# A chunked recurrence with routing beside it: update and bonus ahead of the state's product, logits a step later, the zero fill in four parts

## The chip, the cores and the metric

The kernel runs on 1 core of one Trainium2 chip. The metric is the device time of one execution in microseconds; the time before is the median of three runs. One execution was also profiled, and its trace is what is read below.

## The reference

Three layers follow each other, all in fp32. The first is a linear recurrence over 768 time steps for 4 batches and 8 heads of 48 dimensions:

```python
for t in range(S):
    cur = np.einsum('bhd,bhe->bhde', u[None] * kt, vt)
    y[:, :, t] = np.einsum('bhd,bhde->bhe', rt, state + cur)
    state = w[None, :, :, None] * state + np.einsum('bhd,bhe->bhde', kt, vt)
```

Its output, as 3072 tokens of 384 values, goes through a routed mixture of 8 experts (a token is computed if its product with w_skip is positive, by the expert with the largest logit, weighted by the softmax's value), and then through a soft mixture: logits x @ phi to 32 slots, a softmax over the tokens to gather slot inputs, 8 experts of 4 slots each, and a softmax over the slots to give the result back to the tokens.

## The kernel before, in words

**Steps of the recurrence.** The loop over i from 0 to 23 (L973 to L1047) takes one chunk of 128 tokens of one batch at a time: 6 chunks of time by 4 batches, the batch running faster. All 8 heads are in one step, as 4 pairs, a pair's heads at partitions 0 and 64. The functions below are called with the step whose data they take, j:

- load(j), called three steps ahead: SyncE issues two loads of r and k (rkb, 192 KB each) and one of k and v (kvt, 384 KB), into five buffers each.
- prep(j) and prepk(j), one step ahead: VectorE scales r and k (rks, L616), GpSimd makes their product pd (L618) and the decayed keys kt (L624).
- scores(j): TensorE multiplies keys and queries into sc (L633), a PSUM tile with one buffer, and sums pd over the head into dt (L636); ScalarE copies dt to dts (L638). These are the bonus rows, the term with u.
- inter(j), a step late: TensorE multiplies the queries with the state, which ScalarE has laid out as sbd (stateb, L676), into yp (L702).
- trx(j), two steps late: TensorE transposes the finished y (yt) through the same PSUM tag "t" that dt uses (L721); ScalarE copies it to x (L722), the token-major table.
- bonus(j): TensorE transposes dts (L656) into the PSUM tile ud, one buffer, which also holds the update and the routing's sums.
- upd(j): TensorE forms keys times values, the chunk's addition to the state (L649), into ud. There is none for the last time chunk, steps 20 to 23.
- amask(j): VectorE masks sc into at (L681) and copies the bonus rows onto its diagonal (copy_predicated, L688).
- state(j): VectorE adds the update to the decayed state (L668; GpSimd has made the decayed state, L667).
- av(j), a step late: TensorE multiplies at with the values into yp (L712); ScalarE copies it to yt (L715).

**Routing.** Every four steps a group of four tiles (all batches of a time chunk) is finished and is routed during the following steps, with rc, rb = divmod(i - 5, 4). At rb 0 route1 multiplies yt with the gate, skip and phi weights (lgt, L744) and ScalarE copies the logits; at rb 1 route2 transposes them (lgp, L804) and route2b finds the chosen expert with eight small VectorE operations (L820 to L837) and ScalarE's exponential (L831); at rb 3 route3 counts tokens with six small matmuls into ud, weave and count compute gate weights and places (VectorE, L861 to L888), and route4 stores the logits of the soft mixture: lt on GpSimd, and ltm with the maximum's negative as bias on ScalarE (mn, L905, and four activations, L907). scat(j) is GpSimd's indirect DMA of x rows to the experts' buffer xs_d. At steps 21 to 23 the maximum of ltm over the tokens is taken (cmax, colmax, the matmul of rows), subtracted (lx, L1007, L1029) and exponentiated (L1030). Groups of the last steps follow behind the loop.

**Order.** The schedule is manual: every engine executes its instructions in the order in which the code issues them. SyncE's queue also issues the zero fill of xs_d (L1034, one DMA of 3096 KB at step 2) and the experts' weights (wload at steps 8, 11 and 14, two of 768 KB each).

**Behind the recurrence.** The experts (L1119 on) load rows of xs_d, transpose them and run in fp32 parts on TensorE (L1140 to L1167) until some 350 us; the soft mixture follows.

Of the kernel before, what the change touches and what calls it, by code (L numbers as in the profile page):

```python
# [19 lines left out]
P = 128  # L20
NC_ = S // P
NT = B * NC_
DM = H * D
# [438 lines left out]
def tile_main(ctx, tc, rk, kv, wu, wcat, phi, w1, w2, v1, v2, r_in, k_in, v_in, w_in, u_in, wcn, out, dbg=None, force=False):  # L462
# [92 lines left out]
    def constants(i):  # L555
        if i == 3:
            nc.vector.tensor_scalar(tri, mask, float(E), None, op0=ALU.mult)
        if i == 4:
            nc.vector.tensor_scalar(eb2[0:1], eb_i[0:1], 1.0 / E, None, op0=ALU.mult)
            nc.vector.memset(eb2[32:33], -float(NOROW // E))  # L560
            nc.vector.tensor_scalar(w8, eb_i, -1.0, float(E), op0=ALU.mult, op1=ALU.add)
        if i == 5:
            nc.vector.memset(x[:, :, DM : DM + 1], 1.0)
            nc.vector.memset(ohacc, 0.0)
        if i == 6:
            nc.vector.tensor_reduce(sel4, ident.rearrange("p (q s) -> p s q", q=4), axis=AX.X, op=ALU.add)
            nc.vector.tensor_scalar(pio, pi_i, float(E), None, op0=ALU.mult)

# [57 lines left out]
    def scores(j):  # L626
# [11 lines left out]
        nc.scalar.copy(t["dts"], dt_)  # L638

    def upd(j):  # L640
        t = T[j]
# [9 lines left out]
    def bonus(j):  # L651
        t = T[j]
        t["ud"] = ps.tile([P, 352], F32, tag="ud", name=f"ud{j}")
        t["dk"] = t["ud"][:, 0 : P + 4 * E]
        t["dtk"] = t["ud"][:, 0:P]
        nc.tensor.transpose(t["dtk"], t["dts"], ident)  # L656

# [240 lines left out]
    def route4(g):  # L898
        c, (j0, nb) = g, GR[g]
        sh = [P, nb, E]  # L900
        r = RT.pop(c)
        lg, m = r["lg"], r["m"]
        nc.gpsimd.tensor_copy(lt[:, j0 : j0 + nb, :], lg[:, :, 9:41])
        mn = rt.tile([P, nb, 1], F32, tag="mn", name=f"mn{c}")
        nc.scalar.mul(mn, m, NEG)  # L905
        for b in range(nb):
            nc.scalar.activation(ltm[:, j0 + b, :], lg[:, b, 9:41], AF.Identity, bias=mn[:, b, :])  # L907

# [63 lines left out]
    if True:  # L972
        for i in range(NT):  # L973
# [4 lines left out]
            if i == 0:  # L978
                prep(0)
                for hf in range(2):  # L980
                    r0 = 64 * hf
                    nc.vector.tensor_copy(usel[r0 : r0 + D, :, hf : hf + 1], wt[r0 : r0 + D, 1, :].rearrange("p (a o) -> p a o", o=1))
            scores(i)
            if i > 0:
                inter(i - 1)
                stateb(i - 1)
            if i > 1:
                trx(i - 2)
            bonus(i)
            if i == 0:  # L990
# [5 lines left out]
                for b in range(B):  # L996
                    nc.gpsimd.memset(sbd[b], 0.0)
            elif i + 1 < NT:
                prep(i + 1)
                prepk(i + 1)  # L1000
            if rok and rb == 1:
                route2(rc)
            if rok and (rb == 3 or i == 23):
                route3(rc, place=T[i]["dk"][:, P:])
            if i == 22:
                mrt = rows(nc, cn, "t", rt, pa, "u", mcs[:, 0:1])
                nc.vector.tensor_copy(lx[:, 0:1, :], mrt)  # L1007
            upd(i)
            amask(i)
            state(i)  # L1010
            if i > 0:
                av(i - 1)
            if rok and rb == 0:
                route1(rc)
            if i == 23:
                route1(5)
            if rok and rb == 1:
                route2b(rc)
            if i == 23:
                weave("gpgpgp", g=gates(4), p=places(4))  # L1020
            if rok and rb == 3:
                weave("gpgpgp", g=gates(rc), p=places(rc))
                count(rc)
                route4(rc)
            if i == 21:
                nc.vector.tensor_reduce(cmax, ltm[:, 0:16, :].rearrange("t b s -> t s b"), axis=AX.X, op=ALU.max)
                colmax(nc, cn, "t", pa, "u", mcs[:, 0:1], fourfold(nc, "t", rt, cmax))
            if i == 22:
                nc.vector.tensor_sub(ltm[:, 0:16, :], ltm[:, 0:16, :], lx[:, 0:1, :].to_broadcast([P, 16, 32]))  # L1029
                nc.scalar.activation(ltm[:, 0:16, :], ltm[:, 0:16, :], AF.Exp)  # L1030
            if i in (8, 11, 14):
                wload((i - 8) // 3)
            if i == 2:
                nc.sync.dma_start(out=xs_d.rearrange("(a p) n -> p a n", p=P), in_=zt.rearrange("p (o n) -> p o n", o=1).to_broadcast([P, NSLOT // P, XW]))  # L1034
            if 3 <= i < 7:
                constants(i)
            if i == 4:
                nc.gpsimd.tensor_copy(x[:, :, DM + 2 : DM + 3].bitcast(I32), row_i.rearrange("p (j o) -> p j o", o=1))
            if i == 6:
                wok = rt.tile([PR, 4], F32, tag="wok", name="wok")  # L1040
# [3 lines left out]
                wmn = mk.tile([PR, 1], BF16, name="wmn")  # L1044
                nc.vector.tensor_reduce(wmn, wok2, axis=AX.X, op=ALU.min)
            if i > 8:
                scat(i - 9)  # L1047
# [54 lines left out]
        cnt = mk.tile([P, E + 1, 1], F32, name="cnt")  # L1102
        nc.vector.tensor_copy(cnt.rearrange("p e o -> p (e o)"), cntp)
        rst.close()
        pst.close()
# [428 lines left out]
```

## Time and profile before

| what | value |
|---|---|
| median of three runs | 379.0 us (377.95 to 379.61) |
| profiled execution, its own time | 377.18 us |
| its span | 375.4 us |
| mean granted clock of TensorE | 0.958 |
| busy: TensorE, VectorE, ScalarE, GpSimd | 344.7, 250.4, 160.6, 118.8 us |
| moved by DMA | 84.36 MB, 225 GB/s |
| zero fill of xs_d | 1 DMA of 3096 KB |
| first expert matmul (L1140) | 164.51 us |

The profile's page gives sums over the span; a stage is read with the stage table (busy time of each engine in a stretch), the table of waits (an engine's idle time in front of an instruction, put down to what released it) and the timeline (instructions in order of their start, with the idle time before them in brackets). Starts are in us from the beginning of the span.

### The profile page before, as it was taken

What the parts mean: (1) busy time and instruction counts of PE and PEld (TensorE: products, weight loads), DVE (VectorE), ACT (ScalarE), POOL (GpSimd) and SP (SyncE); (2) the same over time, 40 slices, a digit from 0 to 9 for tenths busy, and PEclk for the clock granted to TensorE, in tenths of its full rate; (3) what the DMA queues carried; (4) which work ended last, traced back from release to release, by engine and by line L of the source; (5) the groups of instructions that cost most, each with busy time, mean ns of one, the idle gap of its engine ahead of it and who ended that gap; (6) DMA issues with size and microseconds to landing.
All of it is one profiled execution on the core that took longest, in us unless ns stands there. A gap on an engine that the chain in (4) does not pass through costs nothing. (4 is left out here: it accounts for less than half of the span.)

```text
span 375.4 us, 8403 instructions
## 1 busy us (share of the span) xinstructions
PE 344.7 (92%) x3313; PEld 280.3 (75%) x3313; DVE 250.4 (67%) x496; ACT 160.6 (43%) x357; POOL 118.8 (32%) x149
## 2 busy tenths in 40 slices
PE   8998979999899878899999999999999999999860
PEld 3676866868777566369999999999899999734350
DVE  7895987896969874646748484748565865426660
ACT  1253424444534332425555564645555543311270
POOL 7962846776754505420012020202020202020000
PEclk9999989999999998589999999999999999999995
DMA  7999998699943101296977887777867466849485
GB/s 181 278 329 245 240 296 202 226 223 318 230 125 124 41 2 44 67 320 222 326 269 245 275 272 245 259 262 266 294 239 241 110 233 199 308 148 399 173 315 196
DMA packets 45696, 84.36 MB, mean 225 GB/s; under 512 B 3961, under 2 KB 26831, under 8 KB 45648
## 3 DMA queue, kind: packets, MB, share of 16 engines
q1 hardware_dynamic: 42320, 78.29, 66.6%
q0 software_dynamic: 2800, 5.28, 4.8%
q8 instruction: 28, 0.46, 0.5%
q10 hardware_dynamic: 528, 0.16, 0.2%
q14 instruction: 20, 0.16, 0.1%
HBM read 72.94 MB, written 13.30 MB: 230 GB/s over the span
## 5 line engine op out<-in xcount | busy, mean ns | idle before, releaser
L1140 PE MATMUL hp<-xhl,wa 128*128 128x256 f32 x192 | 48.6, 290 | 0.2 <-ACT xhl L1130 0.2
L1141 PE MATMUL hp<-xhl,wa 128*128 128x256 f32 x192 | 47.2, 282 | 0.0
L1165 PE MATMUL yp<-wb,hh 128*128 128x384 f32 x128 | 45.3, 354 | 0.0
L953 DVE TENSOR_TENSOR wa<-w,wa 128x768 fp32r<-128x768 f32 x32 | 30.5, 954 | 22.1 <-ACT wa L965 20.9
L1166 PE MATMUL yp<-wb,hh 128*128 128x384 f32 x128 | 43.1, 337 | 0.0
L1167 PE MATMUL yp<-wb,hlo 128*128 128x384 f32 x128 | 43.1, 337 | 0.0
L1198 POOL DMA_INDIRECT lt_d<-lsr,id x16 | 17.5, 1095 | 80.2 <-ACT xhl L1130 56.7
L688 DVE COPY_PREDICATED at<-ident,ud 128x1024 f32<-128x1024 int32 x24 | 31.6, 1315 | 12.1 <-PE ud L649 6.9
L618 POOL TENSOR_TENSOR pd<-rkb 112x512 f32<-112x512 f32 x24 | 30.6, 1277 | 24.8 <-DMA rkb<-in_rk_dram 10.1
L1140 PEld LDWEIGHTS hp<-xhl,wa 128*128 128x128 f32 x192 | 36.4, 189 | 0.5 <-ACT xhl L1130 0.5
L1141 PEld LDWEIGHTS hp<-xhl,wa 128*128 128x128 f32 x192 | 36.5, 190 | 0.0
L891 POOL DMA_INDIRECT xs_d<-x,idx x24 | 24.1, 1004 | 29.2 <-ACT yt L715 12.6
L633 PEld LDWEIGHTS sc<-rks 48*128 48x128 f32 x384 | 23.3, 187 | 13.0 <-DVE at L681 7.9
L633 PE MATMUL sc<-rks 48*128 48x128 f32 x384 | 27.9, 285 | 5.5 <-DVE at L681 5.4
L953 DVE TENSOR_TENSOR wb<-w,wb 128x768 fp32r<-128x768 f32 x32 | 30.5, 954 | 3.2 <-ACT wb L965 3.2
L616 DVE TENSOR_TENSOR rks<-rkb,prk 112x1024 f32<-112x1024 f32 x24 | 29.1, 1213 | 5.2 <-DMA rkb<-in_rk_dram 4.9
L681 DVE TENSOR_TENSOR at<-sc,mask 128x1024 f32<-128x1024 f32 x24 | 29.2, 1218 | 3.0 <-PE sc L633 3.0
L965 ACT CAST wb<-w 128x768 fp32r<-128x768 f32 x32 | 26.8, 838 | 9.0 <-PE yp L1167 5.1
L1150 ACT ACTIVATE hh<-hp 128x512 fp32r<-128x512 f32 x32 | 19.1, 597 | 26.2 <-PE hp L1143 26.2
L1151 DVE SCALAR_TENSOR_TENSOR hlo<-hp,hh 128x512 fp32r<-128x512 f32 x32 | 22.0, 688 | 12.4 <-ACT hh L1150 12.4
L1143 PE MATMUL hp<-xhl,wa 128*128 128x256 f32 x192 | 28.3, 283 | 0.0
L712 PE MATMUL yp<-at,kvt 128*48 128x128 f32 (+1 forms) x384 | 28.0, 281 | 0.0
(330 smaller groups left out, 697.1 us busy)
## 6 DMA issues: line engine op xcount, KB each, us to landing
w<-in_w_dram SPq DMA_DIRECT2D x32, 768.0 KB
v<-in_v_dram SPq DMA_DIRECT2D x29, 768.0 KB
rkb<-in_rk_dram SPq DMA_DIRECT2D x48, 192.0 KB
kvt<-in_kv_dram SPq DMA_DIRECT2D x24, 384.0 KB
out_dram<-ob SPq DMA_DIRECT2D x5, 768.0 KB
xs_d<-zt SPq DMA_DIRECT2D x1, 3096.0 KB
xg<-xs_d POOLq DMA_DIRECT2D x6, 387.0 KB, 5.2
x<-in_v_dram SPq DMA_DIRECT2D x2, 768.0 KB
```

The source lines that it names most:

```text
L616: nc.vector.tensor_mul(rks, rkt, prk)
L618: nc.gpsimd.tensor_mul(t["pd"], rkt[:, 0], rkt[:, 1])
L633: nc.tensor.matmul(sc[:, hf, p, :], ks[r0 : r0 + D, p, :], rs[r0 : r0 + D, p, :], start=True, stop=True)
L681: nc.vector.tensor_mul(at, t["sc"], mask.rearrange("s (a o t) -> s a o t", a=1, o=1).to_broadcast([P, 2, 4, P]))
L688: nc.vector.copy_predicated(at, ident_i.rearrange("s (a o t) -> s a o t", a=1, o=1).to_broadcast([P, 2, 4, P]), t["dtk"].rearrange("s (p o ...
L953: nc.vector.tensor_sub(lv, sl, hv.bitcast(F32))
L1140: nc.tensor.matmul(hp[:, f, :], hi[:, k, fs], xh[:, k, :], start=(k == 0 and f == 0), stop=False)
L1141: nc.tensor.matmul(hp[:, f, :], lo[:, k, fs], xh[:, k, :], start=False, stop=False)
L1143: nc.tensor.matmul(hp[:, f, :], hi[:, k, fs], xl[:, k, :], start=False, stop=(k == 2 and f == 1))
L1165: nc.tensor.matmul(YP[e][bl], hh[:, f, bs], hi[:, f, :], start=st, stop=False)
L1166: nc.tensor.matmul(YP[e][bl], hh[:, f, bs], lo[:, f, :], start=False, stop=False)
L1167: nc.tensor.matmul(YP[e][bl], hlo[:, f, bs], hi[:, f, :], start=False, stop=en)
```

## The change

1. upd and bonus are called right behind scores, ahead of inter, stateb and trx; newud takes the tile. route3 follows bonus, and so does route1.
2. route1 moves from rb 0 to rb 1 and route2 to the end of that step; route2b moves to rb 2; weave and count stay at rb 3; route4 moves to the next step, rb 0 of the following group. The masked logits become one VectorE operation.
3. The zero fill is issued in four parts, at steps 2 to 5.
4. sel4 and pio (constants) move from step 6 to behind the experts' counts, the weight checks (wok, wmn) from step 6 to step 23.
5. Steps 21 to 23: the maximum is taken behind route4 of group 3 and route1 of group 4; rows stands ahead of the mask, its copy behind it, and the subtraction and exponential move from step 22 to step 23.

```diff
--- before.py
+++ after.py
@@ -562,9 +562,6 @@
         if i == 5:
             nc.vector.memset(x[:, :, DM : DM + 1], 1.0)
             nc.vector.memset(ohacc, 0.0)
-        if i == 6:
-            nc.vector.tensor_reduce(sel4, ident.rearrange("p (q s) -> p s q", q=4), axis=AX.X, op=ALU.add)
-            nc.vector.tensor_scalar(pio, pi_i, float(E), None, op0=ALU.mult)
 
     zt = kp.tile([P, XW], F32, name="zt")
     nc.gpsimd.memset(zt, 0.0)
@@ -637,6 +634,12 @@
         t["dts"] = wk.tile([P, P], F32, tag="dts", name=f"dts{j}")
         nc.scalar.copy(t["dts"], dt_)
 
+    def newud(j):
+        t = T[j]
+        t["ud"] = ps.tile([P, 352], F32, tag="ud", name=f"ud{j}")
+        t["dk"] = t["ud"][:, 0 : P + 4 * E]
+        t["dtk"] = t["ud"][:, 0:P]
+
     def upd(j):
         t = T[j]
         if j < NT - B:
@@ -649,11 +652,7 @@
                     nc.tensor.matmul(up[64 * hf : 64 * hf + m, p, :], kt[:, h * D : h * D + m], kvt[:, 1, h * D : h * D + D], start=True, stop=True)
 
     def bonus(j):
-        t = T[j]
-        t["ud"] = ps.tile([P, 352], F32, tag="ud", name=f"ud{j}")
-        t["dk"] = t["ud"][:, 0 : P + 4 * E]
-        t["dtk"] = t["ud"][:, 0:P]
-        nc.tensor.transpose(t["dtk"], t["dts"], ident)
+        nc.tensor.transpose(T[j]["dtk"], T[j]["dts"], ident)
 
     def state(j):
         if j >= NT - B:
@@ -896,15 +895,11 @@
         tc.add_to_no_dep_group("rows", ins.ins)
 
     def route4(g):
-        c, (j0, nb) = g, GR[g]
-        sh = [P, nb, E]
-        r = RT.pop(c)
+        j0, nb = GR[g]
+        r = RT.pop(g)
         lg, m = r["lg"], r["m"]
         nc.gpsimd.tensor_copy(lt[:, j0 : j0 + nb, :], lg[:, :, 9:41])
-        mn = rt.tile([P, nb, 1], F32, tag="mn", name=f"mn{c}")
-        nc.scalar.mul(mn, m, NEG)
-        for b in range(nb):
-            nc.scalar.activation(ltm[:, j0 + b, :], lg[:, b, 9:41], AF.Identity, bias=mn[:, b, :])
+        nc.vector.scalar_tensor_tensor(ltm[:, j0 : j0 + nb, :], m.to_broadcast([P, nb, 32]), NEG, lg[:, :, 9:41], op0=ALU.mult, op1=ALU.add)
 
 
     wraw, WS = {}, {}
@@ -981,12 +976,19 @@
                     r0 = 64 * hf
                     nc.vector.tensor_copy(usel[r0 : r0 + D, :, hf : hf + 1], wt[r0 : r0 + D, 1, :].rearrange("p (a o) -> p a o", o=1))
             scores(i)
+            newud(i)
+            if i > 0:
+                upd(i)
+            bonus(i)
+            if rok and (rb == 3 or i == 23):
+                route3(rc, place=T[i]["dk"][:, P:])
+            if rok and rb == 1 and rc < 4:
+                route1(rc)
             if i > 0:
                 inter(i - 1)
                 stateb(i - 1)
             if i > 1:
                 trx(i - 2)
-            bonus(i)
             if i == 0:
                 decays()
                 warm(ps, "y", 7)
@@ -995,54 +997,55 @@
                 prepk(1)
                 for b in range(B):
                     nc.gpsimd.memset(sbd[b], 0.0)
+                upd(0)
             elif i + 1 < NT:
                 prep(i + 1)
                 prepk(i + 1)
-            if rok and rb == 1:
-                route2(rc)
-            if rok and (rb == 3 or i == 23):
-                route3(rc, place=T[i]["dk"][:, P:])
             if i == 22:
+                route2(4)
                 mrt = rows(nc, cn, "t", rt, pa, "u", mcs[:, 0:1])
+            amask(i)
+            if i == 22:
                 nc.vector.tensor_copy(lx[:, 0:1, :], mrt)
-            upd(i)
-            amask(i)
             state(i)
             if i > 0:
                 av(i - 1)
-            if rok and rb == 0:
-                route1(rc)
+            if i == 21:
+                route4(3)
+                route1(4)
+                nc.vector.tensor_reduce(cmax, ltm[:, 0:16, :].rearrange("t b s -> t s b"), axis=AX.X, op=ALU.max)
+                colmax(nc, cn, "t", pa, "u", mcs[:, 0:1], fourfold(nc, "t", rt, cmax))
+            elif rb == 0 and 1 <= rc < 4:
+                route4(rc - 1)
+            if rok and rb == 1 and rc < 4:
+                route2(rc)
+            if i == 22:
+                route2b(4)
+            if rok and rb == 2 and rc < 4:
+                route2b(rc)
             if i == 23:
                 route1(5)
-            if rok and rb == 1:
-                route2b(rc)
-            if i == 23:
                 weave("gpgpgp", g=gates(4), p=places(4))
-            if rok and rb == 3:
-                weave("gpgpgp", g=gates(rc), p=places(rc))
-                count(rc)
-                route4(rc)
-            if i == 21:
-                nc.vector.tensor_reduce(cmax, ltm[:, 0:16, :].rearrange("t b s -> t s b"), axis=AX.X, op=ALU.max)
-                colmax(nc, cn, "t", pa, "u", mcs[:, 0:1], fourfold(nc, "t", rt, cmax))
-            if i == 22:
                 nc.vector.tensor_sub(ltm[:, 0:16, :], ltm[:, 0:16, :], lx[:, 0:1, :].to_broadcast([P, 16, 32]))
                 nc.scalar.activation(ltm[:, 0:16, :], ltm[:, 0:16, :], AF.Exp)
-            if i in (8, 11, 14):
-                wload((i - 8) // 3)
-            if i == 2:
-                nc.sync.dma_start(out=xs_d.rearrange("(a p) n -> p a n", p=P), in_=zt.rearrange("p (o n) -> p o n", o=1).to_broadcast([P, NSLOT // P, XW]))
-            if 3 <= i < 7:
-                constants(i)
-            if i == 4:
-                nc.gpsimd.tensor_copy(x[:, :, DM + 2 : DM + 3].bitcast(I32), row_i.rearrange("p (j o) -> p j o", o=1))
-            if i == 6:
                 wok = rt.tile([PR, 4], F32, tag="wok", name="wok")
                 nc.vector.tensor_scalar(wok, wt[:, 0, :], WLO, None, op0=ALU.is_ge)
                 wok2 = rt.tile([PR, 4], F32, tag="wok", name="wok2")
                 nc.vector.scalar_tensor_tensor(wok2, wt[:, 0, :], WHI, wok, op0=ALU.is_le, op1=ALU.mult)
                 wmn = mk.tile([PR, 1], BF16, name="wmn")
                 nc.vector.tensor_reduce(wmn, wok2, axis=AX.X, op=ALU.min)
+            if rok and rb == 3:
+                weave("gpgpgp", g=gates(rc), p=places(rc))
+                count(rc)
+            if i in (8, 11, 14):
+                wload((i - 8) // 3)
+            if 2 <= i < 6:
+                q = NSLOT // 4
+                nc.sync.dma_start(out=xs_d[(i - 2) * q : (i - 1) * q].rearrange("(a p) n -> p a n", p=P), in_=zt.rearrange("p (o n) -> p o n", o=1).to_broadcast([P, q // P, XW]))
+            if 3 <= i < 7:
+                constants(i)
+            if i == 4:
+                nc.gpsimd.tensor_copy(x[:, :, DM + 2 : DM + 3].bitcast(I32), row_i.rearrange("p (j o) -> p j o", o=1))
             if i > 8:
                 scat(i - 9)
         for j in range(15, 20):
@@ -1101,6 +1104,8 @@
         nc.tensor.matmul(cntp[:, E : E + 1], ones[:PR, :], wmn, start=True, stop=True)
         cnt = mk.tile([P, E + 1, 1], F32, name="cnt")
         nc.vector.tensor_copy(cnt.rearrange("p e o -> p (e o)"), cntp)
+        nc.vector.tensor_reduce(sel4, ident.rearrange("p (q s) -> p s q", q=4), axis=AX.X, op=ALU.add)
+        nc.vector.tensor_scalar(pio, pi_i, float(E), None, op0=ALU.mult)
         rst.close()
         pst.close()
         pl = qst.enter_context(tc.tile_pool(name="pl", bufs=1, space=PSUM))
```

**Where instructions move.** TensorE in step 14, before, up to the first two of the update's eight matmuls. The number in a name is its step; sc are the scores, dt the bonus sums, yp the state's product, trp the transposes of y, ud the bonus (from dts) and the update (from kt), lgp the transposes of the logits.

```order
L633 MATMUL sc14_1248<-rks14_1204 128x128 x8
L636 MATMUL dt14_1257<-pd14_1206,usel_120 32x128 x4
L702 MATMUL yp13_1264<-rks13_1115,sbd1_193 112x128 x4
L721 MATMUL trp12_1271<-ident_126,yt3_1232 128x112 x4
L656 MATMUL ud14_1277<-ident_126,dts14_1262 128x128
L804 MATMUL lgp2_1285<-ident_126,lgs2_1235 128x128 x4
L649 MATMUL ud14_1277<-kvt14_1011,kt14_1208 64x48
L649 MATMUL ud14_1277<-kvt14_1011,kt14_1208 48x48
```

And TensorE in the same step now, from the last two of the update's eight matmuls on; sc14, dt14 and the other six stand right ahead of them, in this order:

```order
L652 MATMUL ud14_1242<-kvt14_988,kt14_1199 64x48
L652 MATMUL ud14_1242<-kvt14_988,kt14_1199 48x48
L655 MATMUL ud14_1242<-ident_126,dts14_1240 128x128
L743 MATMUL lgt2_1252<-yt2_898,wcs_118 64x512 x4
L701 MATMUL yp13_1259<-rks13_1119,sbd1_193 112x128 x4
L720 MATMUL trp12_1266<-ident_126,yt3_1215 128x112 x4
L711 MATMUL yp13_1259<-at13_1201,kvt13_907 48x128 x8
L803 MATMUL lgp2_1293<-ident_126,lgs2_1253 128x128 x4
```

All eight matmuls of the update and the bonus now stand between dt and the state's product yp13; group 2's logits (lgt2) have come from the end of step 13 into step 14, and their transposes from the middle of the step to its end.

ScalarE around the copy of the bonus rows of step 13 (dts13), before:

```order
L715 COPY yt2_910<-yp11_1100 112x4x128
L905 ACTIVATE mn1_1160<-lgp1_963 128x4
L907 ACTIVATE ltt_162<-lg1_968,mn1_1160 128x32 x4
L638 COPY dts13_1187<-dt13_1182 128x128
L676 COPY sbd0_192<-sp0_188 48x4x48 x2
L722 COPY x_159<-trp11_1196 128x384
```

And now:

```order
L714 COPY yt2_898<-yp11_1106 112x4x128
L635 COPY dts13_1170<-dt13_1165 128x128
L675 COPY sbd0_192<-sp0_188 48x4x48 x2
L721 COPY x_159<-trp11_1189 128x384
L714 COPY yt3_1215<-yp12_1182 112x4x128
```

mn and the four masked logits no longer stand ahead of dts13; they are one VectorE operation at the end of step 13.

SyncE's queue from the loads of step 5 on (rkb and kvt; kvt's number is its step), before:

```order
L503 DMA rkb0_106<-in_rk_dram 48x1024 x2
L505 DMA kvt5_335<-in_kv_dram 128x768
L1034 DMA xs_d_124<-zt_167 128x16x387
L503 DMA rkb1_107<-in_rk_dram 48x1024 x2
L505 DMA kvt6_398<-in_kv_dram 128x768
L503 DMA rkb2_108<-in_rk_dram 48x1024 x2
L505 DMA kvt7_461<-in_kv_dram 128x768
L503 DMA rkb3_109<-in_rk_dram 48x1024 x2
```

And now:

```order
L503 DMA rkb0_106<-in_rk_dram 48x1024 x2
L505 DMA kvt5_335<-in_kv_dram 128x768
L1044 DMA xs_d_124<-zt_167 128x4x387
L503 DMA rkb1_107<-in_rk_dram 48x1024 x2
L505 DMA kvt6_398<-in_kv_dram 128x768
L1044 DMA xs_d_124<-zt_167 128x4x387
L503 DMA rkb2_108<-in_rk_dram 48x1024 x2
L505 DMA kvt7_462<-in_kv_dram 128x768
L1044 DMA xs_d_124<-zt_167 128x4x387
L503 DMA rkb3_109<-in_rk_dram 48x1024 x2
L505 DMA kvt8_531<-in_kv_dram 128x768
L1044 DMA xs_d_124<-zt_167 128x4x387
```

The zero fill xs_d, 16 blocks in one DMA, is four DMAs of 4 blocks, each with one step's loads behind it.

## Rows read from the trace of the kernel before

Columns of a stage table's row: stretch, its us; busy us of PE, PEld, DVE, ACT and POOL, each with the number of its instructions; PEclk, the granted clock; the DMA engines' share; GB/s.

**Rows 1.** Stage table, first scores of steps 5, 9, 17, 19, 22, then experts

```profile
29.48:55.08 25.60, 21.96 (x295) 17.93 (x294) 18.78 (x35) 9.03 (x23) 13.14 (x15) 0.93 1.05 263
55.08:76.92 21.84, 20.59 (x295) 16.61 (x295) 18.04 (x33) 9.94 (x28) 15.45 (x18) 1.00 0.80 214
98.77:110.95 12.18, 11.31 (x151) 8.72 (x150) 8.17 (x16) 5.76 (x17) 8.34 (x10) 1.00 0.60 161
110.95:128.63 17.68, 15.16 (x192) 11.45 (x191) 16.55 (x30) 7.59 (x21) 8.17 (x9) 1.00 0.27 89
128.63:142.49 13.86, 11.76 (x127) 9.30 (x126) 9.11 (x23) 3.71 (x9) 1.58 (x2) 0.88 0.04 14
170.00:350.00 180.00, 180.00 (x1361) 159.33 (x1363) 111.09 (x206) 86.65 (x167) 24.47 (x31) 1.00 0.75 255
```

**Rows 2.** Table of waits, 8 to 165 us: total, times, longest

```profile
PE trp L721 <- ACT dts L638: 5.8, 6, 1.7
PE sc L633 <- DVE at L681: 5.4, 6, 2.1
DVE rks L616 <- DMA rkb<-in_rk_dram: 4.9, 2, 4.2
DVE lx L1007 <- PE mrpt L97: 2.3, 1, 2.3
DVE xhl L1131 <- ACT xhl L1130: 3.6, 1, 3.6
```

**Rows 3.** Timeline, TensorE: start, us, instructions, idle before them; and step 14

```profile
37.33 0.38 PE L633 MATMUL sc<-rks 48*128 48x128 f32 x2 [1.59 <-DVE at L681]
...
48.92 0.38 PE L633 MATMUL sc<-rks 48*128 48x128 f32 x2 [2.05 <-DVE at L681]
...
84.20 1.16 PE L633 MATMUL sc<-rks 48*128 48x128 f32 x16
85.29 0.43 PE L636 MATMUL dt<-pd,usel 112*32 112x128 f32 x8
85.65 1.13 PE L702 MATMUL yp<-rks,sbd 112*112 112x128 f32 x8
...
87.00 0.28 PE L656 MATMUL ud<-ident,dts 128*128 128x128 f32 x1
...
87.64 0.61 PE L649 MATMUL ud<-kvt,kt 128*64 128x48 f32 x15
88.04 0.30 PE L712 MATMUL yp<-at,kvt 128*48 128x128 f32 x1
```

**Rows 4.** Timeline, VectorE's copies of steps 11 and 12, scores of 12

```profile
72.19 0.38 PE L633 MATMUL sc<-rks 48*128 48x128 f32 x2 [0.38 <-DVE at L681]
72.23 1.33 DVE L688 COPY_PREDICATED at<-ident,ud 128x1024 f32<-128x1024 int32 x1
...
76.17 1.32 DVE L688 COPY_PREDICATED at<-ident,ud 128x1024 f32<-128x1024 int32 x1
```

**Rows 5.** Timeline, step 2's bonus rows and those of step 13

```profile
14.04 0.43 PE L636 MATMUL dt<-pd,usel 112*32 112x128 f32 x8
14.53 0.27 ACT L638 COPY dts<-dt 128x128 f32<-128x128 f32 x1 [3.31 <-PE dt L636]
...
79.00 0.17 ACT L905 ACTIVATE mn<-lgp 128x4 f32<-128x4 f32 x1 [1.37 <-DVE ohacc L888]
80.07 0.24 ACT L638 COPY dts<-dt 128x128 f32<-128x128 f32 x1
80.37 0.60 PE L721 MATMUL trp<-ident,yt 112*128 112x112 f32 x4 [0.87 <-ACT dts L638]
```

**Rows 6.** Stage table, three stretches of 33 to 59 us

```profile
33.30:47.30 14.00, 11.98 (x163) 9.18 (x159) 11.44 (x24) 5.36 (x15) 10.41 (x11) 1.00 1.04 239
47.30:58.50 11.20, 8.74 (x107) 7.46 (x107) 9.40 (x18) 3.54 (x13) 4.48 (x7) 0.85 1.03 283
50.60:53.40 2.80, 2.80 (x15) 2.73 (x16) 2.17 (x2) 1.02 (x4) 1.26 (x1) 0.50 1.02 365
```

## What the change was predicted to do

> **What bounds the kernel now.** I read the stage table first [rows 1]. From 170 to 350 us TensorE is busy for 180.00 of 180.00 us: the experts are its own work, which the change leaves alone, so whatever starts them earlier ends the kernel earlier by as much. The recurrence is different. Four of its steps (9 to 12) take 21.84 us with TensorE busy for 20.59 and VectorE for 18.04; TensorE is the bound there, but stands 1.25 us a cycle, and the two cycles from step 9 to 17 take 98.77 − 55.08 = 43.69 us, so the second is like the first. In steps 5 to 8 it is 25.60 us for much the same 295 matmuls.
>
> The table of waits says what TensorE stands for [rows 2]: 5.8 us before the transposes of x, for ScalarE's copy of the bonus rows (dts), and 5.4 us before the scores, for VectorE's mask of the step before (one scores buffer). The timeline shows where. Of the second kind 1.59 us stand before step 6 and 2.05 us before step 8 [rows 3]; behind the first of them VectorE itself had waited 4.2 us for a load [rows 2]. The first kind comes from ScalarE's order: in step 13 its mn waits 1.37 us for VectorE's counting, the masked logits follow, and only then dts at 80.07, for which the transposes stood 0.87 us [rows 5]. A stand has an echo: after the one before step 8 the granted clock is 0.50, the lower level, for the 2.80 us read in that stretch [rows 6]. The stage of step 22 shows 0.88 [rows 1], some 3.3 us at the lower level by the same reading.
>
> **The change part by part.**
>
> *Masked logits on VectorE, a step later.* ScalarE loses five instructions and one wait per group, and dts has nothing ahead of it. The 5.8 us of waits before the transposes go. VectorE gains one operation of 128x128 per group; no row has it, so I bound it between a small operation (0.2) and half a copy of 1.33 us [rows 4] and take 0.3: 4 × 0.3 = 1.2 us on VectorE, off the path as long as it has slack.
>
> *Update and bonus ahead of the state's product.* Nothing is added, but what lay between dt and bonus, 85.65 to 87.00 = 1.35 us [rows 3], no longer covers ScalarE's copy. From dt's start to the end of dts takes 14.53 + 0.27 − 14.04 = 0.76 us, and dt itself issues in 0.36 and the update in 0.40 (87.64 to 88.04) [rows 3, 5]. So the update alone covers it in steps 1 to 19, to within 0.05 us. Steps 20 to 23 have no update: there TensorE stands some 0.4 to 0.5 us each, 1.8 in all, which the stages below carry. The update also writes the one bank "ud", which VectorE's copy and state addition of the step before must have left. It wants to start 85.65 − 84.20 = 1.45 us after the scores [rows 3]. Step 11's copy starts at 72.23 and ends, with 0.3 of the addition, at 73.85, against 72.19 + 1.45 = 73.64: 0.2 late. Step 12's, at 76.17, is done by 77.8 against 76.92 + 1.45 = 78.4: 0.6 early [rows 1, 4]. So a wait of 0 to 0.2 a step; over 20 steps 0 to 4 us, and I take 0.3, since it is late only where TensorE had already stood for VectorE. For the first four steps, whose update now stands behind VectorE's startup work, 0.2. In return the bank is filled earlier, and VectorE, which now waits for it after its mask, has its copy ready sooner.
>
> *Logits a step later.* The logits' matmuls leave the step in which the mask and the routing's small operations follow each other, and lie in the one where VectorE has most to catch up; route2b moves a step on. VectorE's work per cycle becomes 18.0 + 0.3 = 18.3 us, against 20.6 of TensorE [rows 1]. A VectorE step without routing takes 76.17 − 72.23 = 3.94 us [rows 4], so four leave 18.0 − 15.8 = 2.3 us of small operations, in two steps now. It may fall behind there by 2.3 less two times some 0.45, about 1.4 us. I expect TensorE's stands of 1.25 a cycle to go.
>
> *Zero fill in four parts.* SP issues three more DMAs, the same 3096 KB. Today it is one block, ahead of the loads of step 6 on, which is why VectorE waited 4.2 us for a load and TensorE 1.59 behind it. Now each part stands ahead of one load only. What the queues must move does not shrink: three steps of 786 KB loads × 3, two expert weights of 768 KB and some 0.6 MB of scattered rows are 4.5 MB. At 283 GB/s, the rate from 47.3 to 58.5 us [rows 6], that takes 15.9 us, at 239 GB/s (33.3 to 47.3) 18.8 us, where three steps at the new pace give 15.5. A load leaves two steps (10 us) before VectorE needs it and takes 3, so at least 4 us of lead are there to use. Over three such groups the better rate costs 0 and the worse 10 − 4 = 6 us. I take 0.7, near the better, because the stretch behind the first weights ran at 365 GB/s [rows 6].
>
> *Moved constants, weight checks.* 1.2 us of VectorE (an estimate) leave steps 6 and 7 and come after the counts, where VectorE waits 3.6 us for ScalarE anyway [rows 2]; if that cover is gone, it costs 1.2. The three checks go to step 23: 0.5 us at most.
>
> *Step 21 to 23.* The maximum's matmul, for which VectorE stood 2.3 us [rows 2], moves to where the result is used later, and the subtraction and exponential leave ScalarE's way to dts.
>
> **The sum**, stage by stage against [rows 1], each at TensorE's own work:
> - steps 5 to 8: 25.60 → 20.6, gain 5.0 (1.59 and 2.05 of stands, 1.36 of work at the lower clock);
> - two cycles to step 17: 2 × 1.25 = 2.5;
> - steps 17 and 18: 12.18 → 11.31, 0.9;
> - steps 19 to 21: VectorE is busy 16.55 of 17.68 there, gains an operation and keeps its maximum; 0.2;
> - steps 22, 23: 2.10 us idle and 1.6 lost to the clock, of which I book 1.7, for the new stands come here.
>
> Together 10.3, less 0.2, 0.3 and 0.7: **9.1, say 9.0 us**. The profiled run took 377.2, so it would take 368.2. The median of the runs shown, 379.0, lies 1.8 above it: **370.0 us**.
>
> **A rule that speaks against the split.** The rows first: the one block delayed a load by 4.2 us [rows 2]. If the parts keep half of that delay among them, some 2 us of the 5.0 in steps 5 to 8 stay, and the time is 372; I give this 0.06, inside the forecast's chance below. The Trainium skill, DMA: Bandwidth & Descriptors, section Bandwidth, asks for transfers of at least 1 MiB, and its section on the anatomy of one DMA gives about 2.0 us fixed for each; the parts have 0.79 MB. By that page three more DMAs would be an estimated 6 us of queue time. The trace speaks against it: the weights of step 8 on (48.92 us) are 768 KB each, and the highest rate read, 365 GB/s, stands right behind them [rows 3, 6].
>
> **The rivals.**
>
> A. *The queues become the bound.* DMA engines show a share of 1.03 to 1.06 in steps 5 to 8 [rows 1, 6]; a recurrence that runs faster asks for the same bytes sooner. At the worse rate 6 us stop TensorE (above), and the gain is 3: 376. With half of it, 373. For: the share. Against: 0.60 and 0.80 in other stages. I give it 0.17, at 373 to 377.
>
> B. *Slower: TensorE stops right behind dt in every step.* Inter and trx, 1.35 us [rows 3], used to run before anything needed bank "ud" or dts; now all of it stands behind two waits in program order. If VectorE releases the bank late, that holds the update, then the bonus, then the rest. It decides from the point where its addition ends, step for step, over 2 us after the next scores begin (1.45 are wanted): 0.55 us × 20 steps = 11 us, against 9.0 gained: 381. For: step 11's row, late by 0.2. Against: step 12's, and 2.3 us of slack per cycle. 0.07.
>
> C. *The stands only move.* VectorE has 18.3 of 20.6; if its two crowded steps put the same stands before the scores of the next, only steps 5 and 6 and the end gain, and new stands of 1.8 take that back: 377 to 380. 0.10.
>
> **How the numbers follow.** The forecast gets 0.66 (368 to 373; its low end, 366.5, is a sum of 12.3 us, with the bank, queue and startup waits at nothing and the clock's loss in steps 22 and 23 back in full). A measurement of this kernel tells 0.5%, 1.9 us, from no change. Faster by more: the forecast and nearly all of A, 0.82; within: C and the end of A, 0.11; slower: B, 0.07. The range 366.5 to 376.5 leaves out B, most of C and the end of A.
>
> **What would show it.** Right: the wait of the transposes for dts gone from the table of waits; four steps in 20.6 to 21 us; no granted clock of 0.50 near 50 us; the loads of step 6 on without a stretch of 4 us; the first expert matmul some 9 us earlier. Wrong: TensorE waiting for VectorE's state addition before the update, or for dts before the bonus, over 0.3 us in steps with an update (B); the wait of rks for loads over 5 us (A); the wait of the scores for the mask still at 5 us (C).

## The result and the profile after

The changed kernel takes 368.2 us (median of 4 runs, 366.43 to 369.43) against 378.48 us (4 runs, 377.38 to 379.61) for the kernel before: a ratio of 0.9725, 95% interval 0.9674 to 0.9776, so 2.2 to 3.3% faster. 370.0 was forecast, in a range of 366.5 to 376.5. The profiled execution took 368.21 us, its span 366.5, its clock 0.973.

The stage table of the changed kernel, cut at the first scores of steps 0, 5, 9, 13, 17, 19 and 22, at the state's product of step 23 and at the first expert matmul; the rows from 31.08 to 134.34 answer to [rows 1]:

```profile
8.08:31.08 23.00, 21.47 (x304) 15.71 (x304) 20.37 (x26) 7.72 (x20) 17.00 (x21) 1.00 1.04 273
31.08:52.23 21.15, 21.15 (x297) 16.67 (x295) 17.01 (x27) 9.22 (x23) 11.48 (x14) 1.00 1.03 281
52.23:73.37 21.14, 21.14 (x296) 16.66 (x294) 18.35 (x34) 9.23 (x23) 15.31 (x17) 1.00 0.95 257
...
73.37:94.71 21.34, 21.21 (x296) 16.66 (x295) 18.45 (x35) 9.23 (x23) 12.84 (x14) 1.00 1.03 262
...
94.71:106.49 11.78, 11.78 (x153) 8.71 (x151) 10.53 (x20) 5.12 (x12) 9.78 (x12) 1.00 0.87 209
106.49:123.31 16.82, 15.08 (x192) 11.37 (x191) 14.01 (x28) 6.17 (x17) 8.71 (x9) 1.00 0.32 95
123.31:134.34 11.03, 10.02 (x127) 8.09 (x126) 9.62 (x26) 3.59 (x9) 0.71 (x2) 1.00 0.03 10
134.34:155.39 21.05, 17.09 (x153) 9.23 (x151) 11.69 (x55) 8.01 (x20) 9.52 (x13) 0.76 0.28 88
```

From step 5 to step 18 TensorE is now busy for practically all of the time, at a granted clock of 1.00. Steps 5 to 8 fell from 25.60 to 21.15 us. The first experts start at 155.39 instead of 164.51 us, 9.1 earlier, and the span is 8.9 shorter.

The table of waits of the changed kernel, 8 to 165 us, the rows of TensorE inside the recurrence and two of VectorE (total, times, longest):

```profile
PE ud L655 <- ACT dts L635: 2.1, 5, 0.4
PE lgt L743 <- DVE ltt L902: 0.9, 1, 0.9
PE ud L652 <- POOL kt L621: 0.7, 1, 0.7
PE ud L652 <- DVE sp L663: 0.4, 1, 0.4
DVE rks L613 <- DMA rkb<-in_rk_dram: 1.5, 1, 1.5
DVE at L687 <- PE ud L652: 0.7, 1, 0.7
```

The 5.8 and 5.4 us of [rows 2] are gone. In their place the bonus waits 0.4 us for ScalarE's copy in five steps, step 0 and steps 20 to 23, and the update waits once for the decayed keys (0.7, in step 0) and once for VectorE's addition (0.4, in step 1). The stand of 0.9 us ahead of the logits is in step 21, behind the masked logits that are now VectorE's (ltt).

### The profile page after: what moved, and what is told of

Read it like the earlier page. It is cut to its first block, busy times and chain, and to the rows that moved or that the text cites. A ratio compares the mean times of both kernels' runs of the same rounds, so it can differ in the third digit from the quotient of the medians.

```text
span 366.5 us, 8404 instructions
## 1 busy us (share of the span) xinstructions
PE 342.5 (93%) x3313; PEld 277.7 (76%) x3313; DVE 251.0 (68%) x500; ACT 157.6 (43%) x337; POOL 118.1 (32%) x149
## 5 line engine op out<-in xcount | busy, mean ns | idle before, releaser
L960 ACT CAST wa<-w 128x768 fp32r<-128x768 f32 x32 | 26.9, 841 | 0.0
L1170 PEld LDWEIGHTS yp<-wb,hh 128*128 128x128 f32 x128 | 24.1, 188 | 3.5 <-issue 3.5
```

The source lines that it names most:

```text
L960: nc.scalar.copy(hv, sl)
L1170: nc.tensor.matmul(YP[e][bl], hh[:, f, bs], hi[:, f, :], start=st, stop=False)
```

## The experiments

Twelve runs follow; one of them is the changed kernel again (y1), and two are of one and the same kernel (x9 and y2). Their whole times are not to be compared across chips: the part from the state's product of step 23 to the first expert matmul, in which they run the same instructions but for two small constants on VectorE, took between 16.1 and 22.0 us (last section). So the table below gives the stages of the recurrence, cut as above, from one trace of each, then that part ("behind"), and the ratio of the whole time to that of the kernel before on the same chip. Times in us.

| kernel | steps 0–4 | 5–8 | 9–12 | 13–16 | 17, 18 | 19–21 | 22, 23 | behind | ratio (95%) |
|---|---|---|---|---|---|---|---|---|---|
| before | 21.39 | 25.60 | 21.84 | 21.85 | 12.18 | 17.68 | 13.86 | 22.02 | 1 |
| changed, first trace | 23.00 | 21.15 | 21.14 | 21.34 | 11.78 | 16.82 | 11.03 | 21.05 | 0.9725 (0.967–0.978) |
| changed again (y1) | 22.47 | 21.15 | 21.14 | 21.15 | 11.78 | 16.84 | 11.04 | 19.49 | 0.9765 (0.972–0.981) |
| one fill (x1) | 22.47 | 26.43 | 21.14 | 21.15 | 11.78 | 16.84 | 11.04 | 20.87 | 0.9828 (0.976–0.990) |
| fill alone (x7) | 21.40 | 22.57 | 21.81 | 21.81 | 12.28 | 16.90 | 13.54 | 16.32 | 0.9890 (0.984–0.994) |
| old order (x2) | 21.39 | 20.79 | 21.90 | 21.88 | 12.52 | 20.04 | 10.13 | 19.27 | 0.9811 (0.972–0.990) |
| bonus between (x3) | 22.18 | 20.94 | 21.29 | 21.28 | 11.89 | 19.09 | 10.11 | 20.77 | 0.9789 (0.973–0.985) |
| logits on ScalarE (x4) | 22.47 | 21.15 | 21.14 | 21.15 | 11.78 | 17.23 | 10.93 | 19.50 | 0.9733 (0.968–0.979) |
| constants back (x8) | 22.66 | 21.15 | 21.14 | 21.15 | 11.83 | 16.85 | 11.03 | 16.05 | 0.9789 (0.976–0.981) |
| old end (x10) | 22.61 | 21.14 | 21.14 | 21.15 | 11.78 | 16.85 | 15.35 | 16.09 | 0.9917 (0.989–0.995) |
| fill and order, old routing (y4) | 22.46 | 25.02 | 20.99 | 21.34 | 11.99 | 16.32 | 16.87 | 19.02 | 0.9983 (0.994–1.003) |
| mixed order (y2) | 21.39 | 20.77 | 21.95 | 21.20 | 11.78 | 16.83 | 10.05 | 20.24 | 0.9745 (0.970–0.979) |
| mixed order (x9) | 21.40 | 20.78 | 21.96 | 21.14 | 11.78 | 16.82 | 10.05 | 16.16 | 0.9744 (0.972–0.976) |
| mixed order, logits on ScalarE (y3) | 21.40 | 20.77 | 21.95 | 21.15 | 11.78 | 17.23 | 10.05 | 20.26 | 0.9768 (0.972–0.982) |

The theory: the recurrence had been held by three separate things, the one large fill, the place of update and bonus, and the end of step 22. Its main rivals: the fill is hidden anyway, and the new order costs what it gives.

**The zero fill in one piece again (x1), and in four parts alone (x7).**

```diff
-            if 2 <= i < 6:
-                q = NSLOT // 4
-                nc.sync.dma_start(out=xs_d[(i - 2) * q : (i - 1) * q]...
+            if i == 2:
+                nc.sync.dma_start(out=xs_d.rearrange(...), in_=zt...
```

x1, undoing it in the changed kernel: 

> The changed kernel with the zero fill as one DMA of 3096 KB at step 2 again. If the split took away the long load wait (VectorE 4.2 us, TensorE 1.6 us before step 6), both come back and the time is 1.5 to 2.5 us above the changed kernel's 368.2, about 370. Rival: the new order of the other work leaves enough lead on its own, the wait ends before VectorE needs the load, and the time stays within 0.5 us of 368.2.

Steps 5 to 8 take 26.43 us, 5.3 more; against y1 no other stage of the recurrence moves. The whole took 371.1 us, where x4, whose stages are nearly the changed kernel's, took 366.5 on the same chip. The timeline of x1 (start, us, instruction, idle before it) and a stage row show both halves of it:

```profile
34.79 1.22 DVE L613 TENSOR_TENSOR rks<-rkb,prk 112x1024 f32<-112x1024 f32 x1 [4.01 <-DMA rkb<-in_rk_dram]
...
37.20 1.11 PE L630 MATMUL sc<-rks 48*128 48x128 f32 x14 [2.01 <-DVE at L680]
```

```profile
37.20:47.61 10.41, 10.25 (x81) 5.93 (x81) 6.61 (x9) 2.49 (x6) 6.10 (x8) 0.67 0.85 199
```

VectorE waits 4.01 us for the load behind the fill and TensorE 2.01 for VectorE. In the step behind that, TensorE is busy for 10.25 of 10.41 us, but at a mean granted clock of 0.67, so partly at the lower of its two levels, and takes 10.41 instead of 7.20 us. The direction was right, the size was not: 1.5 to 2.5 us were expected, and the 3.2 us that the step behind the stand took longer, more than the stand itself, were not.

x7, the same edit alone in the kernel before: 

> The kernel before with the zero fill in four parts and nothing else. If the one large fill alone made steps 5 to 8 long (25.60 us, against 21.15 in the changed kernel), they fall to 21 to 22 us here, and the time falls by 3.5 to 4.5 us, to 373.5 to 374.5. Rival: the 2.05 us ahead of step 8 and the lower clock behind it are VectorE's routing and come all the same; then only the 1.6 us ahead of step 6 go, and the time falls by 1 to 2.

Steps 5 to 8 fall from 25.60 to 22.57, by 3.0. The stand before step 6 is gone (1.6 us). The stand before step 8 stays, behind VectorE's routing and constants of step 7, but the lower clock behind it does not. The scores of step 8 in x7, then step 8 in x7 and in the kernel before:

```profile
47.58 0.60 PE L633 MATMUL sc<-rks 48*128 48x128 f32 x6 [2.33 <-DVE at L681]
```

```profile
47.58:52.19 4.61, 4.61 (x75) 4.06 (x75) 4.46 (x5) 1.44 (x4) 1.93 (x2) 1.00 1.03 309
48.92:55.08 6.16, 6.16 (x75) 5.40 (x75) 4.55 (x5) 1.44 (x4) 1.92 (x2) 0.72 1.05 327
```

So the rival is right about the stand (2.33 us, against 2.05 before) and wrong about the clock: step 8 takes 4.61 instead of 6.16 us. In the kernel before TensorE had also stood 1.59 us before step 6; here it had not. A stand of this length does not bring the lower clock every time, and what decides it stays open. Of the other stages, steps 19 to 21 are 0.8 us shorter and steps 22 and 23 0.3, though the edit does not touch them; with one trace of each kernel, nothing shows whether that is the fill's. The whole is 1.1% faster (0.6 to 1.6%), 4.4 us in the medians, as the theory had it (though not its 21 to 22 us for the stage) and more than the rival's 1 to 2.

**Bonus and update at their old places (x2).**

```diff
             scores(i)
-            newud(i)
-            if i > 0:
-                upd(i)
-            bonus(i)
...
             if i > 1:
                 trx(i - 2)
+            newud(i)
+            bonus(i)
...
+            if i > 0:
+                upd(i)
             amask(i)
```

> The changed kernel with bonus and update back at their old places (bonus behind the transposes, update ahead of the mask), routing, fill and the rest as changed. If this order is what took the stands away, VectorE's copy waits for the update again (6.9 us in the kernel before) and TensorE stands before the scores: 371 to 374. Rival: the gain is the routing's and the fill's, and the new order only costs TensorE 0.12 us a step (4.57 instead of 4.45): about 366.

Both hold, in different stages, and the whole time, 370.1 us, lies between the two (x4 took 366.5 on the same chip). Where VectorE has routing to do, the old order costs: 0.75 us in each cycle, 0.7 in steps 17 and 18, 3.2 in steps 19 to 21. Where it has none, the old order is cheaper: 1.1 us in steps 0 to 4 (against y1), 0.4 in steps 5 to 8, 0.9 at the end; its plain step takes 4.47 us, against 4.57. The sum to the state's product of step 23 is 3.1 us in favour of the new order (2.4 against the first trace). The 3.2 us in steps 19 to 21 are not the old order's alone: with the old routing it takes 16.90 there (x7). It is the later routing together with the old order that costs them. The table of waits of x2, 8 to 165 us, says how: VectorE's copy waits for the update again, and TensorE for VectorE.

```profile
DVE at L687 <- PE ud L652: 13.1, 9, 2.2
PE lgt L743 <- DVE ltt L902: 3.4, 4, 2.4
PE sc L630 <- DVE at L680: 3.3, 6, 0.9
```

**The bonus behind the state's product (x3).**

```diff
             if i > 0:
                 upd(i)
-            bonus(i)
...
                 inter(i - 1)
                 stateb(i - 1)
+            bonus(i)
             if i > 1:
                 trx(i - 2)
```

> The changed kernel with the bonus behind the state's product instead of ahead of it; the update stays first. If TensorE's step grew from 4.45 to 4.57 us because the bonus waits for ScalarE's copy right behind the update, the step goes back to 4.45 and steps 20 to 23 lose their stands of 0.44: 2 to 4 us faster, 364 to 366. Rival: the update costs more when no matmul with the values follows it, whatever that is; the step stays at 4.57 and only the 0.44 of four steps go, about 366.5 to 368.

The rival is right about the plain step, which does not go back to 4.45: it is 4.61 us (4.57 in the changed kernel). There the cost is the update's place. In the step with the logits it is the bonus's: that step of steps 5 to 8 takes 6.93 us here and 6.92 in x2, against 7.21 in the changed kernel. The timelines of TensorE, first the changed kernel's step 11, then the same step of x3:

```profile
65.45 0.67 PE L652 MATMUL ud<-kvt,kt 128*64 128x48 f32 x16
66.05 0.33 PE L655 MATMUL ud<-ident,dts 128*128 128x128 f32 x1
66.22 1.04 PE L701 MATMUL yp<-rks,sbd 112*112 112x128 f32 x8
67.09 0.55 PE L720 MATMUL trp<-ident,yt 112*128 112x112 f32 x4
```

```profile
64.55 0.67 PE L652 MATMUL ud<-kvt,kt 128*64 128x48 f32 x16
65.14 1.13 PE L701 MATMUL yp<-rks,sbd 112*112 112x128 f32 x8
```

From the update's start to the start of what follows it are 0.60 us when that is the bonus and 0.59 when it is the state's product, against 0.40 when it is the product of mask and values (87.64 to 88.04, [rows 3]). Steps 22 and 23 lose their stands (0.9 us), as both forecasts had it. In steps 19 to 21 x3 loses 2.3 us: the logits of step 21 wait 2.4 for VectorE, whose copy waits 10.3 us in all, over the whole recurrence, for the later bonus (in the changed kernel 0.7 for the update and 0.2 for the bonus). The whole is no faster: 368.6 us, against 366.5 for x4 on the same chip. So the early bonus lets VectorE's copy start right behind its mask, and that pays where VectorE is crowded.

**The masked logits on ScalarE at the later place (x4).**

```diff
-        nc.vector.scalar_tensor_tensor(ltm[:, j0 : j0 + nb, :], ...
+        mn = rt.tile([P, nb, 1], F32, tag="mn", name=f"mn{g}")
+        nc.scalar.mul(mn, m, NEG)
+        for b in range(nb):
+            nc.scalar.activation(ltm[:, j0 + b, :], lg[:, b, 9:41], AF.Identity, bias=mn[:, b, :])
```

> The changed kernel with the masked logits as five ScalarE instructions again, at their new, later place. If ScalarE's order was the cause of the stands before the transposes, some 1.2 us of ScalarE ahead of dts now stop TensorE before the bonus, 0.5 to 0.9 us for each of four groups: 370 to 371.5. Rival: at the later place their inputs are long there, ScalarE does them in its idle time before dt is ready, and the time stays within 0.5 us of 368.2.

The rival: all stages agree with the changed kernel's to 0.1 us, but for 0.4 in steps 19 to 21. So these instructions are out of the way of dts at the later place on either engine.

**The two constants at step 6 again (x8).** The edit puts the two lines on sel4 and pio back into constants. 

> The changed kernel with the two constants (sel4 and pio, some 1.2 us of VectorE) at step 6 again. VectorE waits 1.9 us in the step with the logits for the scores, and step 6 is such a step: within 0.5 us of the changed kernel, steps 5 to 8 at 21.15. Rival: they make VectorE late for the mask of step 6 and the stand ahead of step 7 or 8 comes back: steps 5 to 8 at 22 or more.

As expected: 21.15 in steps 5 to 8.

**The end of step 22 as before (x10).**

```diff
             if i == 22:
                 route2(4)
                 mrt = rows(...)
-            amask(i)
-            if i == 22:
                 nc.vector.tensor_copy(lx[:, 0:1, :], mrt)
+            amask(i)
...
             if i == 22:
                 route2b(4)
+                nc.vector.tensor_sub(ltm[:, 0:16, :], ...
+                nc.scalar.activation(ltm[:, 0:16, :], ..., AF.Exp)
```

> The changed kernel with the end of step 22 as before: the maximum's copy ahead of the mask, subtraction and exponential at the end of step 22 instead of in step 23. If ScalarE's exponential ahead of dts made the long stand in step 23 (1.68 us and the lower clock behind it in the kernel before), steps 22 and 23 take 12.5 to 14 us again (11.03 in the changed kernel) and the time is 1.5 to 3 us longer. Rival: the stand came from VectorE being late, which the earlier bonus has ended; within 0.5 us.

Steps 22 and 23 take 15.35 us, 4.3 more, beyond the 12.5 to 14 expected; the whole is 4.4 us longer than x8 on the same chip (367.5 against 363.1). The cause named first is right, the size was not. The timeline of x10: ScalarE's exponential, waiting for VectorE's subtraction, is ahead of dts, and the bonus right behind dt now stands 2.68 us; the state's product behind it takes 1.47 instead of 1.11 us, since the clock falls to its lower level there (0.89 over the two steps).

```profile
132.05 0.63 ACT L1024 ACTIVATE ltt<-ltt 128x512 f32<-128x512 f32 x1 [1.15 <-DVE ltt L1023]
132.58 0.25 ACT L635 COPY dts<-dt 128x128 f32<-128x128 f32 x1
132.88 0.33 PE L655 MATMUL ud<-ident,dts 128*128 128x128 f32 x1 [2.68 <-ACT dts L635]
133.20 1.47 PE L701 MATMUL yp<-rks,sbd 112*112 112x128 f32 x8
```

**Fill and order without the later routing (y4).** x7 with newud, upd, bonus and route3 called right behind scores, as in the changed kernel. 

> The kernel before with the zero fill in four parts and update and bonus first, the routing as before. If both parts are needed, the bonus in the steps with masked logits on ScalarE waits for dts (mn waits for VectorE's counting, and is in front of it): 1 to 2 us in one step of four, cycles of 22 us or more, and no faster than the fill alone (21.8). Rival: the order alone takes the stands away and the cycles fall to 21.2 as in the changed kernel.

In the cycles (four steps each, 9 to 12 and 13 to 16) the rival is right: 20.99 and 21.34 us. The bonus waits for dts in them, but little: 0.23 and 0.61 us. In steps 5 to 8 (25.02) and 22, 23 (16.87) the gain is lost. Before step 8 TensorE stands 2.55 us, behind constants and routing of the same step on VectorE, one of which took long:

```profile
44.28 2.58 DVE L567 TENSOR_SCALAR pio<-pi_i 128x2 f32<-128x2 int32 x1
```

The whole is, as the forecast said, no faster than the fill alone: a ratio of 0.9983, against 0.9890 for x7. So the later routing earns nothing in an ordinary cycle; it takes VectorE's routing away from the step in which the constants and weight checks stood. Neither makes the stand before step 8 alone: the routing by itself, in the cycles here, puts no such stand before the scores, and the constants by themselves none in x8; together they make 2.05 (before), 2.33 (x7) and 2.55 us. How much of the 2.55 is the long pio is not shown. The old end is what x10 shows alone.

**A mixed order (x9, and y2 beside the changed kernel, y1).** Old order in steps 0 to 8, new in 9 to 21, in 22 and 23 the update first and the bonus behind the state's product.

```diff
+            old = i < 9
+            end = i > 21
+            if not old:
+                newud(i)
+                upd(i)
+                if not end:
+                    bonus(i)
...
+            if end:
+                bonus(i)
...
+            if old:
+                newud(i)
+                bonus(i)
...
+            if old and i > 0:
+                upd(i)
             amask(i)
```

x9: 

> The changed kernel with the old place of bonus and update in steps 0 to 8, the new one in steps 9 to 21, and in steps 22 and 23 the bonus behind the state's product. If the new order is worth its price only where VectorE has the routing to do, steps 0 to 4 go back to 21.4 us (23.0 in the changed kernel), 5 to 8 to 20.8 (21.15), steps 22 and 23 to 10.1 (11.03), the steps between stay: state's product of step 23 near 131.5 us instead of 134.3, time 365 to 366.5. Rival: VectorE enters step 9 later than it does in the changed kernel, and the cycle behind it takes back what the early steps gave: 367.5 to 368.5.

x9 has the stages expected for steps 0 to 8 and 22, 23, and gives 0.8 us back in steps 9 to 12 (21.96), a part of what its rival said: ratio 0.9744, interval 0.9724 to 0.9763. Its time, 361.29 us, lies below the expected 365 to 366.5 because the part behind the recurrence took 16.2 us on that chip; that part is not the edit's, since the same kernel took 20.2 there in y2.

y1: 

> The changed kernel itself, unchanged, on the chip of this call, as the measure for the three others. Stages as in its first trace: 21.15 us a cycle, 16.8 in steps 19 to 21, 11.0 in steps 22 and 23. What differs from call to call should be the part from the state's product of step 23 to the first expert matmul (21.05 us in its first trace, 16.1 in three kernels of the last call).

y2: 

> The mixed order again (old place of bonus and update in steps 0 to 8, bonus behind the state's product in steps 22 and 23), beside the changed kernel on one chip: 1.5 to 2.5 us below it (early steps 1.3 to 1.6, steps 5 to 8 0.4, end 1.0, less 0.8 in steps 9 to 12). Rival: the end's part does not reach the experts and no more than 1 us is left.

On one chip y1 takes 366.36 (366.14 to 366.51) and y2 365.09 us (364.93 to 367.07): 1.3 us less in the median, under the 1.5 expected. The state's product of step 23 starts at 132.05 instead of 133.97, 1.9 earlier (0.3 of it already ahead of step 0), of which 0.7 are lost behind it (20.24 against 19.49). Its recurrence is the shortest of the study, but the two ratios' intervals overlap and one of its six runs is longer than all of y1's, so that it beats the changed kernel rests on these medians and the stages.

y3, the mixed order with the logits on ScalarE: 

> The mixed order with the masked logits on ScalarE at their later place. If, as the single run of that edit showed, it is the later place that took them out of the way and not the engine, within 0.7 us of the mixed order, and the stand of step 21 (0.9 us for the VectorE operation) is one for ScalarE. Rival: where the bonus stands behind the state's product and VectorE is at its limit, one operation less on VectorE lets steps 9 to 12 be shorter: 1 us faster.

365.86 us (365.44 to 368.4), 0.8 above y2 and so just outside the 0.7; steps 9 to 12 take the same 21.95 and steps 19 to 21 take 0.4 more. The rival falls.

## Why the prediction was right, point by point

The total, 9.0 us, was measured as 10.3 in the medians, 9.0 in the profiled runs and 9.6 with y1. The causes named were the right ones in the main, but the exact total is partly luck: in the traces the recurrence gave 8.1 us, the part behind it another 1.0, and the terms miss in both directions.

- **Steps 5 to 8**: 5.0 less 0.7 for the queues was forecast, 4.45 measured. That the one block held up the loads behind it is shown by x1 and x7; the second stand was VectorE's routing and constants together (x7, x8, y4). The queues did not become the bound (rival A, whose shares of 1.03 to 1.06 are 1.02 to 1.05 in the rows): TensorE is busy for all of these steps, and one wait of 1.5 us for a load is left.
- **The two cycles**: 2.5 forecast, 1.21 measured (1.4 in y1). The stands went, as forecast. The step that failed is "each at TensorE's own work": that work was taken from the old order as fixed, 20.6 us a cycle, and is 21.15 in the new one, 0.14 a step. In a plain step (4.57 us, against 4.47 in x2) that is the update, which takes 0.60 instead of 0.40 us away from the product with the values, while its neighbours win back only a part; in the step with the logits it is 0.2 to 0.3, by the bonus's place (x3). So the sign named for the forecast, four steps in 20.6 to 21 us, was missed by 0.14. Steps 17 and 18 fall short by the same: 0.4 for 0.9.
- **Steps 0 to 4**: 0.2 of loss was forecast, 1.6 measured (1.1 in y1). 0.17 us a step is the update's place again; the rest is the wait for VectorE's addition (0.4) and, in the first trace alone, that for the decayed keys (0.7).
- **Bonus behind dt**: 0.4 to 0.5 in steps 20 to 23 and within 0.05 elsewhere; 0.44 in four steps, and no stand elsewhere from step 1 on. Right.
- **The bank "ud"**: 0.3 forecast, 0.4 once. Rival B did not come: VectorE's copy starts behind its mask, since it no longer waits for the update, and so its addition is early enough. x2 shows the reverse.
- **The masked logits**: the forecast put the 5.8 us down to ScalarE's order, which is right, and to the engine, which x4 contradicts: the later place is enough. Even at the old place, in the new order, they cost only 0.23 and 0.61 us a cycle (y4).
- **Steps 19 to 21**: 0.2 forecast, 0.86 measured. VectorE's busy time there fell from 16.55 to 14.01 us with the routing a step later, but that is not shown to be the gain: x7, with routing and order as before, takes 16.90 us there, within 0.1 of the changed kernel, and y4, with the routing as before, 16.32. Where the 0.8 comes from stays open.
- **Steps 22, 23**: 1.7 forecast of 3.7 possible, 2.83 measured. The forecast took 2.0 us off for the new stands; the two that lie here are 0.44 us each, and the clock's loss came back in full. x10 shows stand and clock return together.
- **Behind the recurrence**: nothing forecast, 1.0 gained in the first trace, from a part that differs by more than that from trace to trace.
- **The rule that spoke against the split**: the parts of 0.79 MB cost nothing that the runs show, and no run shows the estimated 6 us of queue time; steps 5 to 8 ran at 281 GB/s against 263 [rows 1]. The larger transfer was the dearer one here, for what it stood in front of.

## What to carry to other kernels

When a transfer that nobody waits for soon shares a queue with loads, cut it up: its size is a delay for all that is queued behind it, and a stand of 2 us can cost more in the clock behind it than by itself (3.2 us in x1), or nothing there (x7). When instructions are put into another order, read the work's own length anew: a group of small matmuls can be cheaper or dearer by its neighbours. An order that helps where the other engine is crowded can cost where it isn't, so it may be chosen by stage.

## What the runs showed of the hardware

**The part behind the recurrence has two lengths.** In the changed kernel ScalarE's copy of the last y stands 2.65 us for a cause that the trace doesn't name ("remote"), TensorE 2.17 for it, and from 142.5 to 152.5 us the granted clock is at its lower level:

```profile
139.78 0.58 ACT L714 COPY yt<-yp 112x512 f32<-112x512 f32 x1 [2.65 <-remote]
140.42 1.09 PE L763 MATMUL lgp<-wcs,yt 112*128 112x42 f32 x8 [2.17 <-ACT yt L714]
```

```profile
142.50:152.50 10.00, 8.58 (x51) 2.71 (x50) 6.86 (x22) 4.50 (x9) 3.98 (x5) 0.51 0.21 66
```

In x7, x8, x9 and x10, all on one chip, neither stand is there and the part takes 16.1 to 16.3 us; elsewhere it takes 19.0 to 22.0. On that chip the kernel before took 371.2 us in the median, against 375.9 to 378.5 elsewhere. What the copy stands for stays open; no run was made on it.

**A tiny VectorE instruction can take long.** pio, 128x2 from int32 to fp32, took 0.15 to 0.16 us wherever it stood behind the experts' counts, but 0.66 in x8, 0.80 in the kernel before and 2.58 in y4, where it stood at step 6. It is not the conversion: in x7 pio took 0.15 at that place, and the weight check right behind it, fp32 alone and 0.15 or 0.16 us in every other kernel, took 1.25:

```profile
43.54 0.15 DVE L567 TENSOR_SCALAR pio<-pi_i 128x2 f32<-128x2 int32 x1
43.60 1.25 DVE L1042 TENSOR_SCALAR wok<-wt 112x4 f32<-112x4 f32 x1
```

So in all four kernels with the constants at step 6 one of these two instructions was slow, and in none of the others. Why is open.
